# Moving the zero fills to a later pass, packing the routing logits and sharing softmax sums in a fused attention and two feed-forward kernel

## The chip, the cores and the metric

The kernel runs on one core of a Trainium2 chip. The metric is device time in microseconds (us) of one execution, as the median of several. Engines are TensorE (PE; its weight loads are PEld), VectorE (DVE), ScalarE (ACT), GpSimd (POOL) and SyncE (SP), which here only issues DMAs. Each engine works through its own list of instructions in order and waits where one needs something that is not there yet.

## What is computed

```
attn = softmax over the last 64 keys of q k^T / 8;  x = attn v      (4 batches, 8 heads, 576 x 64)
x    = reshaped to 2304 tokens x 512
h    = x w_in;  g = h tanh(softplus(h));  x = g w_out               (512 -> 2048 -> 512)
out  = x;  for tokens with x . w_skip > 0:
       e = argmax(x w_gate) of 8 experts, p its softmax weight
       out += p * relu(x w1[e]) w2[e]                               (512 -> 1024 -> 512)
```

The softmax divides by the sum plus 1e-9, in both places where one is taken.

## The kernel before

The 2304 tokens are six blocks of 384 (`NB`), each of three tiles of 128. A block passes through 16 chunks (`NF`) of the first feed-forward, 96 chunks in all. For chunk c, `L1` (L733) multiplies the block by 128 columns of w_in into an accumulator `ph`; seven small steps on VectorE and ScalarE make g of it (`m_min` L738, `m_exp` L741, `m_square` L745, `m_ln` L751, `m_r` L754, `m_g` L760, then a split into a high and a low part for blocks 1 to 5); `L2` (L784) adds its product with w_out into three accumulators po0, po1, po2, one for each tile. In block 0 the weights are also unpacked and split, by VectorE and ScalarE, and weights of w_out are read back by a DMA (`wide_back`, L677, tile ca). In that stage the attention of block 1 runs too, and so on, one block ahead. The attention of block 0 is the ramp ahead of chunk 0.

Attention goes by pairs of units (24 pairs, 48 units; a pair is two heads of a block): scores `sc` on TensorE (L504, 64x64 quadrants), masked row maxima on VectorE (`att_max`, L518), the sign flip of the maxima (`att_neg`, L523), exponentials with row sums on ScalarE (`att_exp`, L528), an addition and a reciprocal (L532, L535), the normalisation (L544), a transpose on TensorE (`tp`, L549), its copy PT, and the product with v (`pv`, L560). From pair 8 on q and k come transposed by VectorE (`dve_T`, L486 and L487) from tiles rq and rk, which SP loads.

After a block's last L2 its three tiles are evacuated (`x_evac`, L826 or L828) into tiles xs, of which there are three buffers, stored to the output, transposed (`rtp`, L839), copied to xf, and multiplied with [w_gate, w_skip] (`route_lg`, L852: four accumulating matmuls of a 128x128 float32 stationary and nine columns for each tile). `route_lge` (L857) copies the nine logits; the class `Group` makes of them a slot for every token, and an indirect DMA on GpSimd scatters the token to a slot table `xg_d` in DRAM (L272). Before the first scatter that table is filled with zeros: `fill_zero` (L263, L264) makes one zero tile zt in a buffer of the same three as xs, and `fill_store` (L267) stores it 16 times, 257 KB each, from GpSimd's queue. The second feed-forward runs at the end, expert by expert (L1182 to L1243).

The order on every engine comes from a planner (`Plan`). Each piece of work is a task with engines and costs (`one`, `two`), what it must follow (`after`), which buffers it takes (`get`) and uses, and a due time; `chunk_time(c)` is the planned time of chunk c. The planner takes the ready task that can start first and is due first, so a change of one due time or cost moves other instructions too. Tasks of the places below: `fz` and `fs` (zero tile and fills, L955 to L958), `xe` (evacuation), `rT`, `re`, `rl`, `lg` (routing, L975 to L983), `mx`, `ng`, `ex`, `ep`, `rc`, `nm`, `PT` (attention, L609 to L618). In gaps that the planner foresees in the ramp and at the end it puts small matmuls (`keep_warm`, L1136).

Of the kernel before, what the change touches and what calls it, by code (L numbers as in the profile page):

```python
# [169 lines left out]
def tile_kernel(  # L170
# [37 lines left out]
    def ctile(shape, dt, name):  # L208
        return cst.tile(shape, dt, tag=name, name=name)
# [26 lines left out]
    wgs = ctile([128, NK, NE + 1], F32, "wgs")  # L236
# [97 lines left out]
    def expert_L(eng, key):  # L334
# [22 lines left out]
                cv=2, ca=2, u=3, gHL=2, xs=3, xf=1, grp3=1, grp1=3)  # L357
# [4 lines left out]
    def one(eng, cost):  # L362
        return [(eng[0], eng[1], cost)]
# [143 lines left out]
    def att_max(u):  # L507
        sc = sc_t[u]
        first = [3 * g for g, _, _, s0 in runs(u // 8) if s0 == 0]
        if u in EXTRA:  # L510
            P = chp.tile([128, 3, 128], F32, tag="u", name="P", bufs=3)
        else:
            P = atp.tile([128, 3, 128], F32, tag="P", name="P")
        P_t[u] = P
        mx_t[u] = mx = atp.tile([128, 4, 3], F32, tag="mx", name="mx", bufs=4)
        for i in range(3):
            mask = [mask_first[w % 2] for w in first if w // 2 == i] or [maskA]
            V.tensor_tensor_reduce(P[:, i], sc[:, i], mask[0],  # L518
                                   op0=ALU.add, op1=ALU.max, scale=1.0, scalar=-3.0e38,
                                   accum_out=mx[:, 0, i:i + 1])  # L520

    def att_neg(u):
        V.tensor_scalar(mx_t[u][:, 1], mx_t[u][:, 0], -0.125, None, op0=ALU.mult)  # L523

    def att_exp(u):
        P, mx = P_t[u], mx_t[u]
        for i in range(3):
            A.activation(P[:, i], P[:, i], AF.Exp, bias=mx[:, 1, i:i + 1], scale=0.125,  # L528
                         accum_out=mx[:, 2, i:i + 1])

    def att_eps(u):
        V.tensor_scalar(mx_t[u][:, 2], mx_t[u][:, 2], 1e-9, None, op0=ALU.add)  # L532

    def att_rec(u):
        V.reciprocal(mx_t[u][:, 3], mx_t[u][:, 2])  # L535

    def att_norm(eng, u):
        P, mx = P_t[u], mx_t[u]
        if eng is A:
            for i in range(3):  # L540
                A.activation(P[:, i], P[:, i], AF.Copy, scale=mx[:, 3, i:i + 1])
        else:
            r = mx[:, 3].rearrange("p (a o) -> p a o", o=1).to_broadcast([128, 3, 128])
            eng.tensor_tensor(P, P, r, op=ALU.mult)  # L544
# [47 lines left out]
    for pr in range(NU // 2):  # L592
# [16 lines left out]
        for j in range(2):  # L609
            u = 2 * pr + j  # L610
            T(("mx", u), one(VV, .64), lambda e, u=u: att_max(u), after=[("S", pr)], get=[("u" if u in EXTRA else "P", ("P", u))],
              use=[("sc", u)])
            T(("ng", u), one(VV, .07), lambda e, u=u: att_neg(u), after=[("mx", u)])
            T(("ex", u), one(AA, 1.16), lambda e, u=u: att_exp(u), after=[("ng", u)])
            T(("ep", u), one(VV, .07), lambda e, u=u: att_eps(u), after=[("ex", u)])
            T(("rc", u), one(VV, .09), lambda e, u=u: att_rec(u), after=[("ep", u)])
            T(("nm", u), two(1.16, .47), lambda e, u=u: att_norm(e, u), after=[("rc", u)])
            T(("PT", u), one(PP, .36), lambda e, u=u: att_PT(u), after=[("nm", u)] + [("PV", pr - 1)] * (pr > 0),  # L618
              get=[("ps", ("tp", u))],
              use=[("P", u)])  # L620
            T(("Pe", u), two(.38, .47), lambda e, u=u: att_PTe(e, u), after=[("PT", u)], get=[("PT", ("PT", u))],
              use=[("tp", u)])
# [198 lines left out]
    xs_t, xf_t, lg_t, lp_t, sel_t, slot_t = ({} for _ in range(6))  # L821
# [26 lines left out]

    def route_lg(m, t):
        lp_t[m, t] = lp = ps_s.tile([128, NE + 1], F32, tag="ps", name="lp")  # L850
        for kk in range(NK):
            PE.matmul(lp, xf_t[m, t][:, kk], wgs[:, kk], start=kk == 0, stop=kk == NK - 1)  # L852

    def route_lge(m, t):
        if t == 0:
            lg_t[m] = sml.tile([128, 3, NE + 1], F32, tag="lg", name="lg", bufs=1)
        V.tensor_copy(lg_t[m][:, t], lp_t[m, t])  # L857
# [108 lines left out]
    for m in range(NB):  # L966
# [3 lines left out]
        for t in range(3):  # L970
# [422 lines left out]
```

## Time and profile before

| what | value |
|---|---|
| median of 3 runs | 718.08 us (717.58 to 719.88) |
| the profiled execution, its own time | 716.83 us |
| its span, first to last instruction | 715.1 us |
| PE, PEld busy | 689.8, 592.7 us |
| DVE, ACT, POOL busy | 457.0, 390.4, 74.2 us |
| moved by DMA | 92.54 MB |

The span is the time between the first and the last instruction in the trace; the time around it belongs to the start and end of the execution. Busy time of an engine is the union of its instructions' records; records of one engine overlap a little, since the next instruction starts before the last one's end has drained, so a group's cost is read from its start to the start of the next group. The clock is TensorE's granted clock as a share of its upper level, 2.4 GHz; 0.5 is the lower level, 1.2 GHz.

### The profile page before, as it was taken

How to read it: one execution, taken by the hardware profiler on the slowest of the kernel's cores; microseconds unless marked ns; L12 is line 12 of the kernel's file. 1: busy time of each engine (PE TensorE's matmuls, PEld its weight loads, DVE VectorE, ACT ScalarE, POOL GpSimd, SP SyncE). 2: the span in 40 equal slices, each digit the busy share in tenths (PEclk: the TensorE clock that was granted, in tenths of full speed). 3: DMA queues.
4: the chain of work that ended last, by engine and by line, in shares of the span. 5: the costliest groups of instructions: out<-in, count | busy, mean ns of one | idle time of the engine just before them, and what ended most of it. 6: DMA issues, size and time to landing. Idle time of an engine off the chain costs nothing.

```text
span 715.1 us, 13649 instructions
## 1 busy us (share of the span) xinstructions
PE 689.8 (96%) x4904; PEld 592.7 (83%) x4904; DVE 457.0 (64%) x1353; ACT 390.4 (55%) x955; POOL 74.2 (10%) x138
## 2 busy tenths in 40 slices
PE   7999997999999999999999999999989999999995
PEld 7776665688888888888888888889978988898983
DVE  5899995887567656665666745546567363564351
ACT  5887774676566666556666665656544243222130
POOL 2000050000020001000020001002233111020011
PEclk9999998999999999999999999999999999999998
DMA  7889998652122213231210300054464677678100
GB/s 174 209 223 272 289 322 193 146 168 73 37 67 59 63 36 72 49 82 30 47 34 21 96 1 9 18 162 133 132 184 146 200 262 251 233 278 300 60 24 20
DMA packets 141645, 92.54 MB, mean 129 GB/s; under 512 B 110189, under 2 KB 118381, under 8 KB 141568
## 3 DMA queue, kind: packets, MB, share of 16 engines
q1 hardware_dynamic: 137568, 82.90, 41.1%
q0 software_dynamic: 4000, 8.63, 3.5%
q8 instruction: 45, 0.74, 0.4%
q14 instruction: 32, 0.26, 0.1%
HBM read 73.96 MB, written 17.86 MB: 128 GB/s over the span
## 4 chain that ended last, share of the span: by engine, by line
PE 56%; issue 16%; DMA 13%; SPq 7%; DVE 4%; POOL 2%; ACT 1%; POOLq 0%; DVEq 0%; ACTq 0%
PE ph L733 23%; PE po L784 23%; DMA w<-in_moe_w_in_dram 4%; DMA vt<-in_v_dram 4%; DMA st<-in_moe_w_dram 2%; PE pv L560 2%; PE lp L852 2%; POOL out_dram L287 2%; PE sc L504 2%; SPq L406 2%; PE tp L549 1%; DMA ca<-w 1%; SPq L420 1%; PE rtp L839 1%; DMA xg<-xg_d 1%
## 5 line engine op out<-in xcount | busy, mean ns | idle before, releaser
L733 PE MATMUL ph<-xH,w 128*128 128x384 f32 x768 | 222.9, 351 | 3.7 <-DVE g L760 2.1
L784 PE MATMUL po<-w,gH 128*128 128x512 f32 x480 | 153.0, 400 | 0.0
L733 PEld LDWEIGHTS ph<-xH,w 128*128 128x128 f32 x768 | 142.1, 189 | 11.8 <-DVE g L760 4.4
L733 PE MATMUL ph<-xL,w 128*128 128x384 f32 x384 | 130.8, 341 | 0.0
L741 ACT ACTIVATE u<-u 128x384 f32<-128x384 f32 x96 | 50.1, 522 | 115.8 <-DVE u L738 103.1
L784 PEld LDWEIGHTS po<-w,gH 128*128 128x128 f32 x480 | 88.1, 188 | 14.5
L784 PE MATMUL po<-w,gL 128*128 128x512 f32 x240 | 95.1, 396 | 0.3 <-DVE gL L769 0.3
L760 DVE SCALAR_TENSOR_TENSOR u<-u,ph 128x384 f32<-128x384 f32 x80 | 44.1, 551 | 60.9 <-ACT u L754 60.4
L733 PEld LDWEIGHTS ph<-xL,w 128*128 128x128 f32 x384 | 72.8, 190 | 2.0 <-issue 1.1
L738 DVE TENSOR_SCALAR u<-ph 128x384 f32<-128x384 f32 x96 | 53.1, 553 | 20.6 <-PE ph L733 20.0
L1182 PEld LDWEIGHTS ph<-xgT,w 128*128 128x128 f32 x512 | 63.7, 190 | 0.9 <-issue 0.3
L1182 PE MATMUL ph<-xgT,w 128*128 128x144 f32 x512 | 64.1, 286 | 0.2 <-issue 0.2
L528 ACT ACTIVATE P<-P,mx 128x128 f32<-128x128 f32 x144 | 55.7, 388 | 7.3 <-DVE mx L523 7.3
L784 PEld LDWEIGHTS po<-w,gL 128*128 128x128 f32 x240 | 45.1, 188 | 12.5 <-DVE gL L769 1.6
L751 ACT ACTIVATE u<-u 128x384 f32<-128x384 f32 x96 | 50.2, 522 | 2.4
L754 ACT ACTIVATE u<-u 128x384 f32<-128x384 f32 x96 | 50.1, 522 | 2.3
L745 ACT ACTIVATE u<-u 128x384 f32<-128x384 f32 x96 | 50.0, 521 | 2.3
L769 DVE TENSOR_TENSOR gL<-u,gH 128x384 fp32r<-128x384 f32 x80 | 47.5, 593 | 3.7 <-ACT gH L310 1.4
L1209 ACT ACTIVATE hH<-ph 128x288 fp32r<-128x288 f32 x32 | 13.2, 411 | 62.3 <-PE ph L1182 43.4
L784 PE MATMUL po<-w,g 128*128 128x512 f32 x96 | 44.4, 598 | 1.0 <-DVE w L669 1.0
L1226 PE MATMUL po<-w,hH 128*128 128x512 f32 x128 | 42.6, 414 | 0.0
L272 POOL DMA_INDIRECT xg_d<-xs,r_si x18 | 18.5, 1030 | 157.0 <-DVE mx L518 77.0
(149 smaller groups left out, 1028.7 us busy)
## 6 DMA issues: line engine op xcount, KB each, us to landing
st<-in_moe_w_dram SPq DMA_DIRECT2D x64, 256.0 KB
w<-in_moe_w_dram SPq DMA_DIRECT2D x32, 512.0 KB
w<-in_moe_w_in_dram SPq DMA_DIRECT2D x16, 512.0 KB
w<-in_moe_w_out_dram SPq DMA_DIRECT2D x16, 512.0 KB
out_dram<-xs SPq DMA_DIRECT2D x18, 256.0 KB
xg_d<-zt POOLq DMA_DIRECT2D x16, 257.0 KB
xg<-xg_d SPq DMA_DIRECT2D x16, 257.0 KB
ca<-w SPq DMA_DIRECT2D x16, 256.0 KB
```

Of the source, the lines that this page charges most:

```text
L528: A.activation(P[:, i], P[:, i], AF.Exp, bias=mx[:, 1, i:i + 1], scale=0.125, accum_out=mx[:, 2, i:i + 1])
L733: PE.matmul(phs[c], a[:, kk], b[:, kk], start=kk == 0 and n == 0, stop=kk == NK - 1 and n == len(terms) - 1)
L738: V.tensor_scalar(u, phs[c], 20.0, None, op0=ALU.min)
L741: A.activation(us[c], us[c], AF.Exp)
L745: A.activation(us[c], us[c], AF.Square, bias=1.0)
L751: A.activation(us[c], us[c], AF.Ln, scale=0.5, bias=half_t[c])
L754: A.activation(us[c], us[c], AF.Exp, scale=-1.0)
L760: V.scalar_tensor_tensor(o, us[c], 1.0, phs[c], op0=ALU.subtract, op1=ALU.mult)
L769: eng.tensor_tensor(gL, us[c], gH.bitcast(F32), op=ALU.subtract)
L784: PE.matmul(po[m, t], a[:, ts], b, start=f == 0 and n == 0, stop=f == NF - 1 and n == len(terms) - 1)
L1182: PE.matmul(ph[:, i], w1_t[e, kk][:, 128 * f:128 * f + 128], xgT[e][:, kk, :N1], start=kk == 0, stop=kk == NK - 1)
L1226: PE.matmul(po2[e, s], a[:, f, ss], b, start=f == 0 and n == 0, stop=f == 7 and n == 2)
```

## The change

Three things, and the planner's new order that follows from them.

- The zero tile and its 16 fills are due at chunks 17 and 18 and after, where they were due at chunks 11 and 13.
- Routing of blocks 0 to 4: for each tile four matmuls with the stationary weights padded to 32 columns (`wgs`, now 128x4x32, zeroed first) write four column quarters of one tile `lq`, one per slice of 128 features; `route_fewe` copies it out, and for each block three matmuls with a constant `sum4` add the four parts and bring the tokens back to the partitions (`route_sum`). One copy of the logits serves a block. Block 5 keeps the old way.
- Softmax: the masked scores are multiplied by -0.125 and their minimum is taken, so the sign flip is gone; maxima and sums of a pair lie in one tile, and the addition and the reciprocal are made once for the pair.

```
-    wgs = ctile([128, NK, NE + 1], F32, "wgs")
+    wgs = ctile([128, NK, 32], F32, "wgs")
+    G.memset(wgs, 0.0)
+    sum4 = ctile([128, NE + 1], F32, "sum4")
+    for p0 in range(0, 128, 32):
+        G.tensor_copy(sum4[p0:p0 + 32], ident[p0:p0 + 32, p0:p0 + NE + 1])
...
             V.tensor_tensor_reduce(P[:, i], sc[:, i], mask[0],
-                                   op0=ALU.add, op1=ALU.max, scale=1.0, scalar=-3.0e38,
-                                   accum_out=mx[:, 0, i:i + 1])
-    def att_neg(u):
-        V.tensor_scalar(mx_t[u][:, 1], mx_t[u][:, 0], -0.125, None, op0=ALU.mult)
+                                   op0=ALU.add, op1=ALU.min, scale=-0.125, scalar=3.0e38,
+                                   accum_out=mx[:, 0, u % 2, i:i + 1])
...
-            A.activation(P[:, i], P[:, i], AF.Exp, bias=mx[:, 1, i:i + 1], scale=0.125,
-                         accum_out=mx[:, 2, i:i + 1])
+            A.activation(P[:, i], P[:, i], AF.Exp, bias=mx[:, 0, u % 2, i:i + 1], scale=-1.0,
+                         accum_out=mx[:, 1, u % 2, i:i + 1])
-    def att_eps(u):
-        V.tensor_scalar(mx_t[u][:, 2], mx_t[u][:, 2], 1e-9, None, op0=ALU.add)
-    def att_rec(u):
-        V.reciprocal(mx_t[u][:, 3], mx_t[u][:, 2])
+    def att_eps(pr):
+        V.tensor_scalar(mx_t[pr][:, 1], mx_t[pr][:, 1], 1e-9, None, op0=ALU.add)
+    def att_rec(pr):
+        V.reciprocal(mx_t[pr][:, 2], mx_t[pr][:, 1])
...
-            T(("ng", u), one(VV, .07), lambda e, u=u: att_neg(u), after=[("mx", u)])
-            T(("ep", u), one(VV, .07), lambda e, u=u: att_eps(u), after=[("ex", u)])
-            T(("rc", u), one(VV, .09), lambda e, u=u: att_rec(u), after=[("ep", u)])
+        T(("ep", pr), one(VV, .07), lambda e, pr=pr: att_eps(pr), after=[("ex", 2 * pr), ("ex", 2 * pr + 1)])
+        T(("rc", pr), one(VV, .09), lambda e, pr=pr: att_rec(pr), after=[("ep", pr)])
...
+    def route_few(m, t):
+        lq_t[m, t] = lq = ps_s.tile([128, 128], F32, tag="ps", name="lq")
+        for kk in range(NK):
+            PE.matmul(lq[32 * kk:32 * kk + 32], wgs[:, kk], xf_t[m, t][:, kk], start=True, stop=True)
+    def route_fewe(eng, m, t):
+        if t == 0:
+            lq_t[m] = sml.tile([128, 3, 128], F32, tag="lq", name="lqs", bufs=1)
+        copy(eng, lq_t[m][:, t], lq_t[m, t])
+    def route_sum(m):
+        lp_t[m] = lp = ps_s.tile([128, 3, NE + 1], F32, tag="ps", name="lp")
+        for t in range(3):
+            PE.matmul(lp[:, t], lq_t[m][:, t], sum4, start=True, stop=True)
-    def route_lge(m, t):
-        if t == 0:
-            lg_t[m] = sml.tile([128, 3, NE + 1], F32, tag="lg", name="lg", bufs=1)
-        V.tensor_copy(lg_t[m][:, t], lp_t[m, t])
+    def route_lge(m):
+        lg_t[m] = sml.tile([128, 3, NE + 1], F32, tag="lg", name="lg", bufs=1)
+        V.tensor_copy(lg_t[m], lp_t[m])
...
-    T(("fz",), one(VV, .55), lambda e: fill_zero(), get=[("xs", "zt")], due=chunk_time(11), t0=chunk_time(10))
+    T(("fz",), one(VV, .55), lambda e: fill_zero(), get=[("xs", "zt")], due=chunk_time(17), t0=chunk_time(17))
...
-          lat=6, due=chunk_time(13) + 1.0 * n)
+          lat=6, due=chunk_time(18) + 1.0 * n)
```

Where it moves instructions. On VectorE, in block 0's pass, the memset of the zero tile (zt) stood between two steps of the weight unpacking (ca, cv, w) before:

```order
L760 SCALAR_TENSOR_TENSOR g<-u,ph 128x384
L654 SCALAR_TENSOR_TENSOR ca<-w_1438,cv 128x512
L263 MEMSET zt 128x513
L264 MEMSET zt 128x1
L654 SCALAR_TENSOR_TENSOR ca<-w_1303,cv 128x512
L671 ISA ca<-ca,cv 128x1024
```

Now it stands behind the transposes for pair 10 and ahead of the normalisations (P) of a pair whose transposes stand between block 0's last two L2 groups on TensorE:

```order
L742 TENSOR_SCALAR u<-ph 128x384
L490 STREAM_TRANSPOSE kT<-rk 128x448
L491 STREAM_TRANSPOSE qT<-rq 128x384
L535 TENSOR_SCALAR mx<-mx 128x6
L267 MEMSET zt 128x513
L268 MEMSET zt 128x1
L538 RECIPROCAL mx<-mx 128x6
L697 TENSOR_TENSOR w_1914<-ca,w_1914 128x512
L547 TENSOR_TENSOR P<-P,mx 128x384 x2
```

It moved by some 50 instructions, from about chunk 10 to about chunk 15 of block 0. On ScalarE, at the border of blocks 0 and 1, the three evacuations xs stood together before, ahead of chunk 18's four steps on u:

```order
L754 ACTIVATE u<-u 128x384
L826 ACTIVATE xs<-po 128x512 x3
L310 ACTIVATE w_2143<-ca 128x512
L741 ACTIVATE u<-u 128x384
L745 ACTIVATE u<-u 128x384
```

Now the third, whose buffer is that of zt, comes after three exponentials and three of chunk 18's four steps:

```order
L830 ACTIVATE xs<-po 128x512 x2
L314 ACTIVATE w_2101<-ca 128x512
L745 ACTIVATE u<-u 128x384
L749 ACTIVATE u<-u 128x384
L531 ACTIVATE P,mx<-P,mx 128x128 x3
L755 ACTIVATE u<-u 128x384
L830 ACTIVATE xs<-po 128x512
L758 ACTIVATE u<-u 128x384
```

On GpSimd the fills (xg_d<-zt) stood among memsets of v tiles and ahead of the three small copies into xs:

```order
L396 MEMSET vt 64x128
L267 DMA xg_d<-zt 128x514 x15
L471 MEMSET rk 128x64
L830 COPY xs<-tok 128x1 x3
```

Now the copies, which follow the evacuations, come between the fills:

```order
L475 MEMSET rk 128x64
L271 DMA xg_d<-zt 128x514 x11
L834 COPY xs<-tok 128x1
L271 DMA xg_d<-zt 128x514
L834 COPY xs<-tok 128x1
L271 DMA xg_d<-zt 128x514 x4
L834 COPY xs<-tok 128x1
```

So the third copy and the third evacuation are behind all 16 fills, which nothing waited for at that place before.

## Rows read from the trace of the kernel before

**Rows 1.** The page, part 1: busy us, share of the span, instructions.
```profile
PE 689.8 (96%) x4904; PEld 592.7 (83%) x4904; DVE 457.0 (64%) x1353; ACT 390.4 (55%) x955; POOL 74.2 (10%) x138
```

**Rows 2.** Busy time by stage: window, length; PE, PEld, DVE, ACT, POOL; clock, DMA.
```profile
46.00:104.00 58.00, 56.65 (x336) 39.14 (x336) 57.17 (x155) 45.92 (x110) 7.12 (x14) 1.00 0.98 280
104.00:109.00 5.00, 4.56 (x18) 3.32 (x19) 2.13 (x7) 2.20 (x9) 2.21 (x5) 1.00 1.12 305
109.00:122.00 13.00, 8.53 (x69) 7.01 (x68) 7.95 (x16) 5.33 (x11) 0.74 (x5) 0.74 0.81 180
122.00:146.00 24.00, 23.11 (x109) 15.28 (x108) 20.36 (x56) 15.96 (x39) 0.00 (x0) 1.00 0.61 146
146.00:525.00 379.00, 379.00 (x2612) 333.90 (x2611) 242.45 (x770) 231.62 (x578) 30.10 (x49) 1.00 0.26 67
```

**Rows 3.** Waits from 84 to 136 us: us in total, times, longest.
```profile
DVE kT L486 <- DMA rk<-in_k_dram: 5.2, 1, 5.2
```

**Rows 4.** Timeline of VectorE: start, us, instruction, idle time before it.
```profile
111.35 0.65 DVE L486 STREAM_TRANSPOSE kT<-rk 128x448 f32<-128x448 f32 x1 [5.22 <-DMA rk<-in_k_dram]
...
113.01 0.55 DVE L544 TENSOR_TENSOR P<-P,mx 128x384 f32<-128x384 f32 x1
```

**Rows 5.** Timeline of TensorE at the stall.
```profile
109.25 0.49 PE L549 MATMUL tp<-ident,P 128*128 128x128 f32 x3
113.71 0.87 PE L549 MATMUL tp<-ident,P 128*128 128x128 f32 x3 [3.97 <-DVE P L544]
114.23 0.67 PE L733 MATMUL ph<-xH,w 128*128 128x384 f32 x1
...
118.35 1.53 PE L560 MATMUL pv<-PT,vt 128*64 128x64 f32 x24
```

**Rows 6.** The chain of waits: an L2 and an L1 group at full clock.
```profile
143.36 2.57 PE po L784 x6
145.93 2.12 PE ph L733 x12
```

**Rows 7.** Timeline of GpSimd: first and last fill issue, and who waits.
```profile
93.94 0.76 POOL L267 DMA_DIRECT2D xg_d<-zt  x1 [39.00 <-DMA vt<-in_v_dram]
...
106.86 0.54 POOL L267 DMA_DIRECT2D xg_d<-zt  x1 [0.19 <-issue]
...
114.51 0.18 POOL L830 COPY xs<-tok 128x1 int32<-128x1 int32 x1 [2.00 <-DMA xg_d<-zt]
```

**Rows 8.** DMA queues from 88 to 115 us: packets, MB, share of 16 engines.
```profile
q1 hardware_dynamic: 9332, 4.04, 58.9%
q0 software_dynamic: 1280, 4.21, 47.9%
```

**Rows 9.** Timeline of TensorE in block 1: transposes, score and logit groups.
```profile
168.80 0.60 PE L839 MATMUL rtp<-ident,xs 128*128 128x128 f32 x4
169.15 0.71 PE L784 MATMUL po<-w,gH 128*128 128x512 f32 x2
...
171.43 0.89 PE L504 MATMUL sc<-kT,qT 64*64 64x128 f32 x24
172.25 0.44 PE L733 MATMUL ph<-xH,w 128*128 128x384 f32 x1
...
176.58 0.96 PE L852 MATMUL lp<-wgs,xf 128*128 128x9 f32 x8
177.39 0.42 PE L733 MATMUL ph<-xH,w 128*128 128x384 f32 x1
```

**Rows 10.** The tile mx: count, duration ns min/median/max.
```profile
L523 DVE TENSOR_SCALAR mx<-mx x48: 139/161/396, 11.7 to 445.5; 128x3 f32<-128x3 f32 x48
L532 DVE TENSOR_SCALAR mx<-mx x48: 125/163/318, 15.1 to 449.4; 128x3 f32<-128x3 f32 x48
L535 DVE RECIPROCAL mx<-mx x48: 131/176/178, 15.8 to 449.5; 128x3 f32<-128x3 f32 x48
```

**Rows 11.** Groups by line: busy us, mean ns of one score pass.
```profile
L504 PE MATMUL sc<-kT,qT 64*64 64x128 f32 x576 | 21.7, 277 | 1.9 <-ACT qT L310 1.2 <-issue 0.7
```

More of the change, by code (lines that the diff above doesn't have):

```diff
@@ L356, in tile_kernel @@
     BUFS = dict(ps=3, ph=2, po0=1, po1=1, po2=1, rk=4, rq=2, vt=3, kT=2, qT=2, P=2, PT=2, xHL=2,
-                cv=2, ca=2, u=3, gHL=2, xs=3, xf=1, grp3=1, grp1=3)
+                cv=2, ca=2, u=3, gHL=2, xs=3, xf=1, grp3=1, grp1=3, lqs=1)
     plan = Plan(BUFS)
@@ L514, in att_max @@
         P_t[u] = P
-        mx_t[u] = mx = atp.tile([128, 4, 3], F32, tag="mx", name="mx", bufs=4)
+        if u % 2 == 0:
+            mx_t[u // 2] = atp.tile([128, 3, 2, 3], F32, tag="mx", name="mx", bufs=3)
+        mx = mx_t[u // 2]
         for i in range(3):
@@ L612, in tile_kernel @@
               use=[("sc", u)])
-            T(("ng", u), one(VV, .07), lambda e, u=u: att_neg(u), after=[("mx", u)])
-            T(("ex", u), one(AA, 1.16), lambda e, u=u: att_exp(u), after=[("ng", u)])
-            T(("ep", u), one(VV, .07), lambda e, u=u: att_eps(u), after=[("ex", u)])
-            T(("rc", u), one(VV, .09), lambda e, u=u: att_rec(u), after=[("ep", u)])
-            T(("nm", u), two(1.16, .47), lambda e, u=u: att_norm(e, u), after=[("rc", u)])
+            T(("ex", u), one(AA, 1.16), lambda e, u=u: att_exp(u), after=[("mx", u)])
+        T(("ep", pr), one(VV, .07), lambda e, pr=pr: att_eps(pr), after=[("ex", 2 * pr), ("ex", 2 * pr + 1)])
+        T(("rc", pr), one(VV, .09), lambda e, pr=pr: att_rec(pr), after=[("ep", pr)])
+        for j in range(2):
+            u = 2 * pr + j
+            T(("nm", u), two(1.16, .47), lambda e, u=u: att_norm(e, u), after=[("rc", pr)])
             T(("PT", u), one(PP, .36), lambda e, u=u: att_PT(u), after=[("nm", u)] + [("PV", pr - 1)] * (pr > 0),
@@ L818, in tile_kernel @@
               use=[("gHL", c)], due=chunk_time(NC + 1) + LO + .01 * t)
-    xs_t, xf_t, lg_t, lp_t, sel_t, slot_t = ({} for _ in range(6))
+    xs_t, xf_t, lg_t, lp_t, lq_t, sel_t, slot_t = ({} for _ in range(7))
     def x_evac(eng, m, t):
@@ L851, in route_lg @@
         for kk in range(NK):
-            PE.matmul(lp, xf_t[m, t][:, kk], wgs[:, kk], start=kk == 0, stop=kk == NK - 1)
-    def route_lge(m, t):
-        if t == 0:
-            lg_t[m] = sml.tile([128, 3, NE + 1], F32, tag="lg", name="lg", bufs=1)
-        V.tensor_copy(lg_t[m][:, t], lp_t[m, t])
+            PE.matmul(lp, xf_t[m, t][:, kk], wgs[:, kk, :NE + 1], start=kk == 0, stop=kk == NK - 1)
+    def route_lge(m):
+        lg_t[m] = sml.tile([128, 3, NE + 1], F32, tag="lg", name="lg", bufs=1)
+        V.tensor_copy(lg_t[m], lp_t[m])
     class Group:
@@ L978, in tile_kernel @@
               get=[("rk" if last else "xf", ("xf", m, t))], use=[("rtp", m, t)])
+            if not last:
+                T(("rl", m, t), one(PP, .25), lambda e, m=m, t=t: route_few(m, t), after=[("re", m, t), ("wg",)],
+                  get=[("ps", ("lq", m, t))], use=[("xf", m, t)], due=tb + dt * (3 + 2 * t))
+                T(("rq", m, t), two(.22, .19), lambda e, m=m, t=t: route_fewe(e, m, t), after=[("rl", m, t)],
+                  use=[("lq", m, t)], get=[("lqs", ("lqs", m))] if t == 0 else ())
+                continue
             T(("rl", m, t), one(PP, .75), lambda e, m=m, t=t: route_lg(m, t), after=[("re", m, t), ("wg",)],
               get=[("ps", ("lp", m, t))], use=[("xf", m, t)], due=tb + dt * (3 + 2 * t))
-            if not last:
-                T(("lg", m, t), one(VV, .08), lambda e, m=m, t=t: route_lge(m, t), after=[("rl", m, t)],
-                  use=[("lp", m, t)])
+        if not last:
+            T(("rs", m), one(PP, .66), lambda e, m=m: route_sum(m), after=[("rq", m, t) for t in range(3)],
+              get=[("ps", ("lp", m))], use=[("lqs", m)], due=tb + dt * 8.5)
+            T(("lg", m), one(VV, .1), lambda e, m=m: route_lge(m), after=[("rs", m)], use=[("lp", m)])
         prev = None
@@ L986, in tile_kernel @@
             g = Group(m, t0, n)
-            lgs = [("lg", m, t0 + t) if n > 1 else ("rl", m, t0) for t in range(n)]
+            lgs = [("lg", m) if n > 1 else ("rl", m, t0)]
             lu = [("lp", m, t0)] if n == 1 else []
```

8 lines of the change are left out of this document (4 added, 4 removed).

## Prediction

> **What bounds the kernel now.** I read the engines' busy time first, then busy time by stage, then the waits of the worst stage, then single instructions there. TensorE is busy for 689.8 us of a span of 715.1 [rows 1]. By stage the picture splits [rows 2]: from 146 to 525 us (blocks 1 to 5 of the first feed-forward) TensorE has no gap at all at full clock, while VectorE is busy 64% and ScalarE 61%. What is taken from TensorE there shortens the run one for one; what is taken from the others is worth nothing. From 46 to 104 us (block 0) TensorE, VectorE and the DMA engines are all full (56.7 and 57.2 of 58 us, DMA share 0.98): no single engine is the bound. Then the stage breaks: from 104 to 122 us TensorE idles 0.44 + 4.47 us, its clock falls to 0.74 of full speed, and VectorE idles 2.87 + 5.05 us.
>
> Why it breaks is in the waits and the timelines. VectorE stood 5.2 us before its transposes of kT, for the DMA that brings rk [rows 3, 4]. The second normalisation of an attention pair stands behind these transposes in VectorE's order; TensorE, which needs it to transpose P, stood 3.97 us [rows 5]. After that idle time its matmuls ran at half speed: the L1 group that starts at 114.23 and ends at 118.35 took 4.12 us, such a group takes 2.12 at full clock [rows 5, 6]. The DMA was late because the 16 fills of the slot table were issued from 93.94 to 107.4 us, and the next instruction that waits for the last of them ran at 114.51 [rows 7]; of the DMA time between 88 and 115 us the fills took 47.9%, everything else 58.9% [rows 8].
>
> **The change part by part.** The sum is made against the profiled execution: span 715.1, time 716.83. The median of the three runs, 718.08, is 1.25 above it; I add that at the end.
>
> *Fills leave block 0.* They are now issued after a memset near the end of block 0's pass, 16 issues on GpSimd's queue as before. What they leave behind is the broken stretch. TensorE idled 4.47 us from 109 to 122 and lost (1 - 0.74) x 13 = 3.4 us to the clock; with the small gaps on either side (0.44 and 0.89) that is 9.2 us at most [rows 2]. VectorE could give back the 7.9 us that it idled. Not all of it returns, for VectorE is full before and 85% busy after (20.36 of 24 us [rows 2]); its order becomes the next thing that is late. I take 7 us, with 3.5 (half) and 9.2 as ends.
>
> *Fills arrive at the border of blocks 0 and 1.* The zero tile takes one of three buffers; the third evacuation of block 0's output needs that same buffer and waits for all 16 fills. It stands in ScalarE's order between two steps of chunk 18, and TensorE's L2 of chunk 16 needs the accumulator that it frees. From the memset's end TensorE has this to do before it stands there: about 2 us until both normalisations are done (0.55 each [rows 4] and two shorter instructions), six transposes 0.8 (0.49 for three [rows 5]), L1 2.12, a pv group 0.9, L2 2.57, L1 2.12, a score group 0.82, L1 2.12, transposes 0.35, two thirds of an L2, 1.4: 15.2 us [rows 6, 9], the pv group priced like a score group's record. The pv group waits for two copies that stand behind four activations of chunk 16 on ScalarE; I put 1.5 us on that. So TensorE arrives after some 16.7 us, and with 0.6 for the evacuation the fills must have landed by 16. Before they took 20.6 us from first issue to release [rows 7]; their packets alone need 0.479 x 27 = 12.9 us of the DMA engines [rows 8], and others use 0.61 of them in the stage that precedes the border [rows 2]. I take 18 us: 2 us late, 1.5 for the pv group, 0.5 for the queue behind. Cost 4 us; ends 0 (landing by 14) and 9.5 (landing after 20.6, 4.6 us idle, with 3.4 us of slow clock behind it as now, and the 1.5). GpSimd has nothing else due then; the loads on SP's queue share the DMA with the fills, and their covers are conversions placed some four chunks ahead of their use.
>
> *Routing.* A tile's four logit matmuls (eight passes) hold TensorE 0.81 us: start 176.58, next group 177.39 [rows 9]. There are 15 such tiles in blocks 0 to 4, all in the full stage: 12.15 us go. Instead each tile has four matmuls of 32 columns on four column quarters (eight passes of 128 moving columns), and each block three summing matmuls (six passes of the old kind, 0.1 each): 5 x 0.6 = 3.0 us. No column quarter is in the trace. Nearest is the score group on 64x64 quadrants, four at a time: 24 passes in 0.82 us [rows 9], 0.034 a pass, so 0.27 a tile. The other end is no overlap, at the rate of the transposes of 128 columns, 0.35 for four [rows 9], 0.7 a tile. I take 0.35, near the quadrants, as they are the same kind of sharing: 15 x 0.35 + 3.0 - 12.15 = -3.9 us; ends -5.1 and +1.35. The Trainium skill ("TensorEngine Tiling (Array Packing)", Key Properties) speaks against the change: a switch of tiling mode drains the engine, and every new group switches twice. The score group's 0.82 already holds two switches, so by the row they cost little; if each had to be paid on top, at the 0.15 us by which the record of an old logit group outlasts its 0.81, the sum would be 15 x 0.57 + 3.0 - 12.15 = -0.6 instead of -5.1. Evacuating the quarters (128x128, on ScalarE or VectorE) is covered by the 36 to 39% that these idle there.
>
> *Softmax.* Per pair of units two sign flips, one addition and one reciprocal leave VectorE: 96 instructions in all, of 0.16 to 0.18 us each [rows 10], overlapping. Sixteen of the 24 pairs run where TensorE is full and VectorE is not: worth nothing. In the ramp and block 0 there are at most 4 x 4 in a stage, 16 x 0.16 = 2.6 us of VectorE time beside full TensorE. The price is that the first unit's sum waits for the second unit's exponentials. I take -0.3 us, for ramp and block 0 together; ends -1 and +1. The extra memset and copies at the start are on GpSimd, before it is waited for.
>
> Sum: -7 + 4 - 3.9 - 0.3 = -7.2. Profiled 709.6, median 718.08 - 7.2 = **710.9**.
>
> **The rivals.** A run of this kernel can tell about 0.3% from no change: 715.9 to 720.2.
>
> (1) *The border costs what block 0 gains.* Fills take their old 20.6 us, TensorE idles over 4 us, the clock falls again: 9.5 instead of 4, 716.4. For it: others already use 0.61 of the DMA, and the old stall of 3.97 us did drop the clock. Against: there are fewer small packets at the border than at 94 us. It decides from a landing some 20 us after the memset. Chance 0.17.
>
> (2) *VectorE is the bound of block 0.* Without the DMA wait TensorE waits for g and for normalisations instead; half returns: 714.4. For it: VectorE has no idle time to speak of from 46 to 104. Against: TensorE has none either. Chance 0.13.
>
> (3) *Everything works.* Fills land in time, quarters overlap like quadrants: -9.2 - 5.1 - 0.3 = -14.6, 703.5. Chance 0.12.
>
> (4) *Quarters do not run side by side*, though the source says so: 0.7 a tile, +1.35 in place of -3.9: 716.1. Chance 0.05.
>
> (5) *Slower:* each pass on a quarter runs to its end before the next starts, at the 0.277 us that a score pass lasts by itself [rows 11]. Then 8 x 0.277 = 2.2 us a tile in the full stage, 15 x 2.216 + 3.0 - 12.15 = +24.1 in place of -3.9: 738.9. It decides from 0.83 us a tile, where the 3.3 us net of the other parts are spent. For it: no row shows matmuls on quarters; against: the score group, whose passes overlap four at a time. Chance 0.05.
>
> **How the numbers follow.** The forecast keeps 0.48. Faster by over 0.3%: forecast, (2), (3) and half of (1), 0.48 + 0.13 + 0.12 + 0.08 = 0.81. Within 0.3%: the other half of (1), and (4): 0.14. Slower: (5), 0.05. The range for 8 in 10 runs from 703.5 (rival 3) to 716.6 (rivals 1 and 4), which leaves out rival 5 and the outer parts of 1 and 3.
>
> **What would show it.** In the changed profile: no wait of VectorE for rk over 1 us near 105 to 112 us, and full clock from 100 to 130; a wait of ScalarE's third xs evacuation for the fills, with TensorE idle 1 to 4 us behind it and the clock at most briefly low; routing groups lq of 0.3 to 0.45 us from start to next start, lp groups of 0.6 per block; the stage of blocks 1 to 5 shorter by 3 to 5 us. Wrong would be: the same idle TensorE in block 0 with no fills near it, a border stall of over 5 us, or lq groups above 0.7 us.

## The result, and the profile after

The changed kernel takes 712.75 us (median of 4 runs, 712.09 to 713.92), the kernel before 718.98 in the same series: ratio 0.9915, 95% interval 0.9888 to 0.9941, 6.2 us faster where 7.2 were forecast (the forecast for the median was 710.9). A second series gave 0.9899 (0.9874 to 0.9924). The profiled execution is one of 712.69 us, span 710.9. The page's part 1, against [rows 1], has 4.5 us less of TensorE and 12.8 less of VectorE:

```profile
PE 685.3 (96%) x4921; PEld 584.8 (82%) x4921; DVE 444.2 (62%) x1247; ACT 396.7 (56%) x973; POOL 76.8 (11%) x144
```

Busy time by stage (columns as in [rows 2]):

```profile
46.00:104.00 58.00, 57.94 (x346) 40.45 (x345) 57.25 (x147) 47.59 (x116) 0.35 (x2) 1.00 0.89 254
104.00:109.00 5.00, 4.70 (x41) 3.25 (x40) 5.00 (x11) 3.37 (x8) 0.00 (x0) 1.00 0.60 143
109.00:122.00 13.00, 13.00 (x72) 8.96 (x71) 12.33 (x35) 9.23 (x25) 0.16 (x1) 1.00 0.69 146
122.00:140.00 18.00, 15.34 (x106) 10.90 (x104) 9.83 (x23) 9.17 (x20) 9.42 (x18) 1.00 0.99 308
140.00:160.00 20.00, 17.85 (x76) 15.67 (x77) 16.64 (x45) 11.19 (x30) 0.34 (x2) 0.83 0.55 176
160.00:515.00 355.00, 355.00 (x2515) 307.21 (x2514) 212.23 (x648) 224.64 (x557) 27.68 (x47) 1.00 0.25 62
515.00:565.00 50.00, 45.69 (x301) 41.66 (x299) 27.51 (x96) 17.49 (x36) 14.54 (x15) 0.93 0.50 165
```

The broken stretch of block 0 is gone: from 104 to 122 us TensorE idles 0.3 us where it idled 4.9, its clock is full, and VectorE is busy 17.33 of 18 us. A new broken stretch stands at the border, 122 to 160 us: TensorE idles 2.66 and 2.15 us, VectorE 8.2 of 18 us and ScalarE 8.8 in the first half, and the clock is 0.83 in the second, a mean of both levels. The waits between 118 and 160 us (us in total, times, longest) say for what:

```profile
DVE w L316 <- DMA ca<-w: 8.2, 3, 4.9
POOL xs L834 <- DMA xg_d<-zt: 7.6, 1, 7.6
ACT w L314 <- DMA ca<-w: 4.5, 2, 4.1
...
PE ph L737 <- DVE u L764: 3.0, 1, 3.0
...
PE po L788 <- ACT xs L830: 1.8, 1, 1.8
```

And the timelines of the four engines there, first VectorE, then ScalarE, TensorE and GpSimd:

```profile
135.28 0.43 DVE L316 CAST w<-ca 128x512 fp32r<-128x512 f32 x1 [4.87 <-DMA ca<-w]
135.63 0.55 DVE L742 TENSOR_SCALAR u<-ph 128x384 f32<-128x384 f32 x1
...
136.21 0.53 ACT L745 ACTIVATE u<-u 128x384 f32<-128x384 f32 x1 [6.39 <-DVE u L742]
...
143.74 0.63 ACT L314 ACTIVATE w<-ca 128x512 fp32r<-128x512 f32 x1 [4.14 <-DMA ca<-w]
...
147.31 0.57 ACT L830 ACTIVATE xs<-po 128x512 f32<-128x512 f32 x1
...
140.37 0.44 PE L737 MATMUL ph<-xH,w 128*128 128x384 f32 x1 [3.03 <-DVE u L764]
...
147.94 1.12 PE L788 MATMUL po<-w,gH 128*128 128x512 f32 x2 [1.78 <-ACT xs L830]
...
151.69 0.63 PE L788 MATMUL po<-w,gH 128*128 128x512 f32 x2
...
134.10 0.54 POOL L271 DMA_DIRECT2D xg_d<-zt  x1 [0.17 <-issue]
142.22 0.18 POOL L834 COPY xs<-tok 128x1 int32<-128x1 int32 x1 [7.58 <-DMA xg_d<-zt]
```

Read them from VectorE on. It stands 4.87 us for a read-back of w_out (tile ca), then makes the first step of chunk 17 (L742); ScalarE has waited 6.39 us for that step; TensorE waits 3.03 us for the g that comes out of the chain. Then ScalarE itself stands 4.14 us for another read-back, and its third evacuation, which comes behind, runs at 147.31. The fills had landed 5 us earlier: the copy that waits for them runs at 142.22, 19.3 us after the zero tile's memset ended (122.95). So what came late was not what the forecast had pointed at: no row has ScalarE waiting for the fills. After the two stops the L2 pairs at 147.94 take twice what the pair at 151.69 takes (1.12 and 0.63). The late reads were slow from issue to landing: of the 16 read-backs issued between 88 and 165 us half landed within 2.4 us, and the slowest took 9.6. The reason is the one that [rows 8] gave for rk: from 122 to 146 us the fills hold half of the DMA time (packets, MB, share):

```profile
q0 software_dynamic: 1280, 4.21, 49.3%
q1 hardware_dynamic: 5856, 2.79, 41.6%
```

Routing, against [rows 9]: a tile's logit group takes 0.36 us to the next start where it took 0.81, the three summing matmuls 0.69:

```profile
162.43 0.43 PE L857 MATMUL lq<-xf,wgs 128*32 128x128 f32 x8
162.79 0.44 PE L737 MATMUL ph<-xH,w 128*128 128x384 f32 x1
...
189.40 0.84 PE L868 MATMUL lp<-sum,lqs 128*128 128x9 f32 x6
190.09 0.42 PE L737 MATMUL ph<-xH,w 128*128 128x384 f32 x1
```

There is one new loss that no step of the forecast named, at the end of the first feed-forward. ScalarE stands for st, the staged weights of the second feed-forward, with the steps of a u behind it, and TensorE waits 3.04 us, then runs its next group slowly:

```profile
530.79 0.63 ACT L314 ACTIVATE w<-st 128x512 fp32r<-128x512 f32 x1 [6.59 <-DMA st<-in_moe_w_dram]
...
534.13 2.07 PE L1062 MATMUL sel<-ident,base 128*128 128x128 f32 x8 [3.04 <-DVE u L764]
```

**A table by stage.** Up to the end of a block every kernel of this study has nearly the same work behind it on TensorE, so the stages can be divided at the L2 groups of the last chunk of a block: the start of whatever follows that group on TensorE. In the timeline after, L2 of chunk 15 starts at 131.57 and the next group at 133.85. The last column is what is left of the span; the ratio is that to the kernel before, with its interval, each in its own series.

| kernel | ratio (95%) | to the end of L2(0) | to L2(15): block 0 | to L2(31): border and block 1 | to L2(79): blocks 2 to 4 | rest |
|---|---|---|---|---|---|---|
| before | 1 | 50.7 | 94.6 | 82.1 | 246.2 | 241.5 |
| the change | 0.9915 (0.9888 to 0.9941) | 49.5 | 84.3 | 89.7 | 244.0 | 243.3 |
| e0, the change again | 0.9899 (0.9874 to 0.9924) | 51.5 | 84.2 | 88.6 | 244.0 | 245.8 |
| e1, fills alone | 1.0014 (0.9998 to 1.003) | 51.2 | 91.4 | 89.4 | 246.2 | 239.8 |
| e2, routing alone | 0.9951 (0.993 to 0.9972) | 50.6 | 94.5 | 81.4 | 244.0 | 242.2 |
| e3, softmax alone | 0.9992 (0.9975 to 1.0008) | 51.7 | 94.7 | 82.1 | 246.1 | 240.6 |
| e4, change, fills back | 0.9967 (0.995 to 0.9984) | 50.7 | 92.9 | 81.4 | 244.0 | 243.4 |
| e5, zero tile in xf | 0.9908 (0.988 to 0.9935) | 53.3 | 84.1 | 88.4 | 244.2 | 245.6 |
| e6, and fills late | 0.9838 (0.9809 to 0.9867) | 53.8 | 84.2 | 83.1 | 244.1 | 242.4 |
| e7, lq twice | 0.9947 (0.9928 to 0.9967) | 50.0 | 84.4 | 88.9 | 246.0 | 244.8 |
| e8, before, fills late | 0.9866 (0.9844 to 0.9888) | 51.1 | 86.6 | 82.0 | 246.2 | 242.6 |
| e9, late, behind routing | 0.9839 (0.9809 to 0.9868) | 53.1 | 84.2 | 81.6 | 244.2 | 244.5 |
| e10, late, 32 fills | 1.0325 (1.0301 to 1.035) | 52.2 | 84.2 | 81.6 | 282.8 | 241.5 |
| e11, late, 24 fills | 0.9826 (0.9788 to 0.9863) | 51.8 | 84.2 | 81.6 | 244.2 | 242.8 |

The three middle columns repeat to some tenths of a us between kernels that share the part in question, except where fills stand at the border; the first and the last differ by 2 to 2.5 us between two executions of the same kernel (the change and e0), so nothing under 2 us is read from a single pair there. The trace of the kernel before is of an execution that took 716.83 us, 1 to 3 us under the medians of its series; where stages add up to less than the ratios say (in e8 6.6 against 9.6 us), this is part of it.

### The profile page after: what moved, and what is told of

The parts are those of the page before. It is cut to its first block, busy times and chain, and to the rows that moved or that the text cites. A ratio compares the mean times of both kernels' runs of the same rounds, so it can differ in the third digit from the quotient of the medians.

```text
span 710.9 us, 13617 instructions
## 1 busy us (share of the span) xinstructions
PE 685.3 (96%) x4921; PEld 584.8 (82%) x4921; DVE 444.2 (62%) x1247; ACT 396.7 (56%) x973; POOL 76.8 (11%) x144
## 4 chain that ended last, share of the span: by engine, by line
PE 76%; issue 7%; DMA 6%; DVE 4%; ACT 2%; SPq 2%; POOL 1%; POOLq 0%; DVEq 0%; ACTq 0%
PE po L788 27%; PE ph L737 26%; PE ph L1209 7%; PE po L1253 4%; PE sc L508 2%; PE pv L563 2%; DMA ca<-w 2%; DMA st<-in_moe_w_dram 2%; PE tp L552 2%; DMA w<-in_moe_w_in_dram 1%; PE rtp L843 1%; DMA vt<-in_v_dram 1%; PE po L1268 1%; PE lq L857 1%; POOL out_dram L291 1%
## 5 line engine op out<-in xcount | busy, mean ns | idle before, releaser
L788 PE MATMUL po<-w,gH 128*128 128x512 f32 x480 | 154.7, 404 | 1.8 <-ACT xs L830 1.8
L745 ACT ACTIVATE u<-u 128x384 f32<-128x384 f32 x96 | 50.0, 521 | 94.7 <-DVE u L742 94.6
L742 DVE TENSOR_SCALAR u<-ph 128x384 f32<-128x384 f32 x96 | 53.0, 553 | 25.9 <-PE ph L737 25.7
L788 PEld LDWEIGHTS po<-w,gL 128*128 128x128 f32 x240 | 45.7, 190 | 11.6 <-DVE gL L773 0.7
```

The lines of the kernel that those rows point to most:

```text
L742: V.tensor_scalar(u, phs[c], 20.0, None, op0=ALU.min)
L745: A.activation(us[c], us[c], AF.Exp)
L788: PE.matmul(po[m, t], a[:, ts], b, start=f == 0 and n == 0, stop=f == NF - 1 and n == len(terms) - 1)
```

## The experiments

**Each part alone.** e1 is the kernel before with the two due times of the change; e2 with its routing, e3 with its softmax; e4 is the change with the due times of before.

```
-    T(("fz",), ..., due=chunk_time(11), t0=chunk_time(10))
+    T(("fz",), ..., due=chunk_time(17), t0=chunk_time(17))
-          lat=6, due=chunk_time(13) + 1.0 * n)
+          lat=6, due=chunk_time(18) + 1.0 * n)
```

> The kernel before with the due times of the zero tile and the fills of the change, nothing else. My theory: the stall of block 0 is the fills' alone, and the price at the border is the fills' too. Then L2 of chunk 15 ends 8 to 11 us earlier than before (145.4 there), TensorE idles 4 to 6 us between chunks 15 and 19 with a slow clock behind it, and some 2 to 3 us of gain are left: ratio 0.996 to 0.998. Rival: the stall of block 0 went because the softmax lost 96 instructions of VectorE in the change; then VectorE is late here without a DMA, L2 of chunk 15 ends at most 5 us earlier, the border is paid in full, and the kernel is slower by 2 to 5 us: ratio 1.003 to 1.007.

It came out between the two, with no difference that is clear of noise (1.0014, interval 0.9998 to 1.003). TensorE stood twice at the border, each time behind VectorE's waits for read-backs, and the first of these stops comes right behind L2 of chunk 15, so the table counts it with block 0. Without its 3.02 us block 0 gave back 6.2 (94.6 to 88.4), and the border took 10.3 (82.1 to 89.4, and those 3.02):

```profile
142.65 0.59 PE L733 MATMUL ph<-xH,w 128*128 128x384 f32 x1 [3.02 <-DVE u L760]
...
150.77 0.69 PE L733 MATMUL ph<-xH,w 128*128 128x384 f32 x1 [4.21 <-DVE u L760]
```

> The kernel before with the routing of the change, nothing else. My theory: TensorE has no gap from 146 to 525 us, so its own time counts one for one: an lq group 0.36 us, three summing matmuls 0.67 per block, 12.97 us of lp groups gone: -4.3 us, ratio 0.994, with the wait of VectorE for rk near 111 us as before. Rival: the gain in the full stage is given back by another order of VectorE and ScalarE at the end of the first feed-forward, as the wait of 3 us ahead of the sel matmuls in the changed kernel suggests: -1 to -2 us, ratio 0.997 to 0.999.

Ratio 0.9951: 3.5 us. 0.7 us of it are in block 1 (82.1 to 81.4) and 2.2 in blocks 2 to 4 (246.2 to 244.0), some 0.73 us a block, and the stall of block 0 is as it was:

```profile
114.65 0.52 PE L553 MATMUL tp<-ident,P 128*128 128x128 f32 x3 [4.67 <-DVE P L548]
```

The rival has something too: the rest does not get shorter though block 4's routing lies there (241.5, 242.2), and TensorE waits 2.72 us ahead of sel, as after the change.

> The kernel before with the softmax of the change, nothing else. My theory: worth 1.2 us in the ramp (the first L1 group starts at 44.73 in the changed kernel and at 45.95 before) and nothing behind it; the wait for rk near 111 us and TensorE's stall there stay: -0.3 to -1.5 us, ratio 0.998 to 1.000. Rival: the normalisation that is now made for a pair is what freed block 0; then the stall of 3.97 us before the transposes of P is gone here too, with the clock full, and the ratio is 0.988 to 0.992.

0.9992, no measurable gain, and block 0 takes 94.7 us as before. But the stall is not the same one. Up to L2 of chunk 9 this kernel needs 51.6 us from L2(0), the one before 53.7, so the softmax does save 2.1 us there. Then the L2 of chunk 12 waits 6.75 us for its weights (w, the last step of their unpacking on VectorE), where before the transposes of P waited 3.97 [rows 5]. The unpacking is late because VectorE stood twice for rk, as it did once before [rows 3], and ScalarE for a read-back:

```profile
114.85 0.65 DVE L486 STREAM_TRANSPOSE kT<-rk 128x448 f32<-128x448 f32 x1 [4.09 <-DMA rk<-in_k_dram]
...
120.23 0.65 DVE L486 STREAM_TRANSPOSE kT<-rk 128x448 f32<-128x448 f32 x1 [3.37 <-DMA rk<-in_k_dram]
...
120.51 0.63 ACT L310 ACTIVATE w<-ca 128x512 fp32r<-128x512 f32 x1 [9.06 <-DMA ca<-w]
...
125.59 4.54 PE L784 MATMUL po<-w,g 128*128 128x512 f32 x6 [6.75 <-DVE w L669]
```

> The changed kernel with the zero tile and the fills due at chunks 11 and 13 again. My theory: the wait for rk comes back near 105 to 112 us (4 to 6 us), the border is clean, and what is left is routing and softmax: 4.3 to 5.5 us faster than the kernel before, ratio 0.992 to 0.994, so that moving the fills is worth no more than 1 to 3 us in the change. Rival: block 0 is freed by routing and softmax, the fills cost nothing there now: 10 us or more faster, ratio 0.986 or less, better than the change.

2.4 us faster than before, less than I expected and far from the rival's 10. Block 0 takes 92.9 us, and the fills still hold it: VectorE's wait for rk is back, 5.76 us, if later than expected, and L2 of chunk 12 waits 5.65 us for the unpacking behind it, as in e3:

```profile
117.47 0.65 DVE L490 STREAM_TRANSPOSE kT<-rk 128x448 f32<-128x448 f32 x1 [5.76 <-DMA rk<-in_k_dram]
...
122.62 4.76 PE L788 MATMUL po<-w,g 128*128 128x512 f32 x6 [5.65 <-DVE w L673]
```

Beside the change (0.9915, 0.9899) the ratio of 0.9967 puts the move of the fills at 3.7 to 4.9 us once routing and softmax are there, more than the 1 to 3 expected. The two traces show only 1.6 of it (spans 712.5 and 710.9; 8.6 won in block 0, 8.3 lost behind it), since e4's is of one of its faster executions (714.25, median 716.86).

**What the border's price is made of.** e5 keeps the fills at the border and takes the shared buffer away: the zero tile goes into the buffer of xf, which is idle until the routing. e6 moves the fills into block 1 as well. e0 is the change itself in the same series.

```
-        zt[0] = xsp.tile([128, XW], F32, tag="xs", name="zt")
+        zt[0] = sml.tile([128, NK * 128 + 2], F32, tag="xf", name="zt", bufs=1)
...
-            xf = sml.tile([128, NK, 128], F32, tag="xf", name="xf", bufs=1)
+            xf = sml.tile([128, NK * 128 + 2], F32, tag="xf", name="xf", bufs=1)[:, :NK * 128].rearrange("p (k n) -> p k n", k=NK)
...
-    T(("fz",), ..., get=[("xs", "zt")], due=chunk_time(17), t0=chunk_time(17))
+    T(("fz",), ..., get=[("xf", "zt")], due=chunk_time(17), t0=chunk_time(17))
```

> The changed kernel itself, unaltered, beside the three that follow. 712 to 714 us, ratio to the kernel before 0.990 to 0.993; in the trace again one idle stretch of TensorE of about 3 us before an L1 group near 140 us and one of 1 to 2.5 us before an L2 group near 148.

As expected in time, and at the lower end in ratio. Its idle stretches were 3.72 and 0.57 us, so the first one repeats and the second, the one that the forecast was about, is the smaller.

> The changed kernel with its zero tile in the buffer of xf (that of the routing, idle then) in place of the third buffer of xs; the fills keep their due times. The third evacuation no longer waits for the fills. My theory: most of the border's price is the read-backs of w_out (ca) that share the DMA engines with the fills; the idle 3 us before the L1 group and the waits of VectorE and ScalarE for ca (8 and 4 us) stay, only the 1.8 us before L2 and some of the slow clock behind it go: 2 to 4 us faster than the change, ratio to before 0.985 to 0.989. Rival: the shared buffer is the price, as the prediction had it; then the border is clean and it is 6 us or more faster than the change, ratio 0.983 or less.

No gain that can be seen: 713.2 beside e0's 713.41, each spread over some 5 us. No evacuation waits for the fills now, and still TensorE stands before an L2 group, because the evacuations come behind chunk 17's steps on ScalarE, and those behind VectorE's wait for a read-back. The waits from 118 to 160 us:

```profile
ACT u L745 <- DVE u L742: 11.1, 5, 7.7
DVE w L316 <- DMA ca<-w: 10.0, 4, 6.2
...
PE po L788 <- ACT xs L830: 4.2, 1, 4.2
```

So the rival, the buffer, falls. My own theory was wrong in size and place: the wait ahead of L1 went, and the one ahead of L2 stayed. In place of two stops of TensorE (3.03 and 1.78 us in the change, 3.72 and 0.57 in e0) there is one of 4.17, behind a wait of VectorE for a read-back that is now 6.2, and the clock from 140 to 160 us is 0.83 again.

In e6 the due times are `chunk_time(24)` for the tile and `chunk_time(25) + 1.0 * n` for the fills.

> The same with the zero tile due at chunk 24 and the fills from chunk 25, in block 1, where the DMA share is 0.25 to 0.3 and no read-back of weights is due. My theory: no stall in block 0 (as in the change), none at the border, and the first scatters move behind the fills at no cost: 6 to 9 us faster than the change, ratio to before 0.978 to 0.983. Rival: wherever 4.2 MB of fills go something waits for them; the scatters hold the three xs tiles until the next block's evacuations (chunk 32), TensorE stands there for 2 us or more, and it is no more than 3 us faster than the change, ratio 0.987 or more.

4.5 us faster than e0 (708.9, 713.41), between theory and rival in time. The border is clean (83.1 against 88.6), and the one idle stretch left is that an xf had to wait for the fills in the buffer that they share:

```profile
180.85 0.43 PE L857 MATMUL lq<-xf,wgs 128*32 128x128 f32 x8 [1.43 <-ACT xf L314]
```

**The fills by themselves.** e8 puts the same late fills into the kernel before, e9 into the change, both with the zero tile made behind block 0's last logit group (`after=[("rl", 0, 2)]` at fz).

> The kernel before, softmax and routing as they were, with the zero tile in the buffer of xf, due at chunk 24 and made behind block 0's last logit group, and the fills from chunk 25. It prices the fills by themselves, at a place where nothing waits for what shares the DMA engines with them. My theory: the stall of block 0 (9 us with its slow clock) is the fills' alone; 6 to 8 us faster than before, ratio 0.989 to 0.992, no wait of TensorE over 2 us between 46 and 200 us. Rival: block 0 needs the softmax of the change too, as the fills alone at the border gave nothing: 0 to 3 us faster, ratio 0.996 or more, with TensorE waiting over 2 us for VectorE or ScalarE in block 0.

Ratio 0.9866, 9.6 us by the ratio, a little over my bound; 8.0 of it in block 0 (94.6 to 86.6), with nothing lost at the border (82.0). The rival falls. Busy time by stage in e8:

```profile
46.00:122.00 76.00, 74.69 (x452) 52.34 (x453) 74.45 (x204) 58.81 (x146) 1.03 (x7) 1.00 0.86 228
122.00:160.00 38.00, 36.92 (x234) 29.03 (x233) 32.90 (x85) 25.82 (x59) 0.35 (x2) 1.00 0.49 142
```

> The late fills of the changed kernel, with the zero tile made behind block 0's last logit group, so that no xf has to wait for the fills (TensorE stood 1.43 us for that). My theory: 0.5 to 2 us faster than that, ratio to before 0.980 to 0.983, no idle TensorE from 120 to 500 us. Rival: the fills, now later, hold up the scatters and with them block 1's evacuations: an idle stretch of 1 us or more near chunk 32 (220 to 230 us), ratio 0.984 or more.

In time it equals e6 (0.9839, 0.9838); in the stage it is 1.5 us shorter (81.6, 83.1), and there is no idle TensorE from 120 to 515 us. It is the kernel to keep: 11.6 us faster than before by the ratio, and some 4.5 faster than the change. Over e8 the ratio gains 2 us, and the two intervals overlap; the three middle stages are 4.8 us shorter, but in these two traces the first stage and the rest are 3.9 longer.

```profile
122.00:160.00 38.00, 38.00 (x245) 30.59 (x246) 32.91 (x89) 26.86 (x69) 0.35 (x2) 1.00 0.53 151
160.00:200.00 40.00, 40.00 (x304) 33.94 (x304) 27.27 (x94) 24.46 (x65) 12.15 (x21) 1.00 0.66 161
200.00:515.00 315.00, 315.00 (x2192) 273.29 (x2187) 187.81 (x562) 198.20 (x489) 25.95 (x42) 1.00 0.25 64
```

**Does block 1 have room?** e10 issues every fill of e9 twice in a row; e11 issues the sixteen and then the first eight again.

> The same with every fill issued twice, 32 in place of 16, the same zeros again. It asks whether the place in block 1 has room or was only just wide enough. My theory: nothing on the path waits for a transfer there, so 4.2 MB more cost 0 to 1 us. Rival: 4.2 MB cost some 5 to 8 us of TensorE at any place where the DMA engines are shared with loads that are needed soon, as in block 0 and at the border; then 4 us or more slower than with 16.

This missed its question. Each second store writes the rows of the one before it and waits for that to land (16 waits, 58.2 us in all), so 32 stores took from 171.67 to 247.57 us, the scatters waited, block 0's xs tiles stayed taken, and TensorE stood 34.02 us for the evacuations of block 1. What it does show is the place's last moment: from 221.2 us on TensorE stands.

```profile
255.22 1.22 PE L789 MATMUL po<-w,gH 128*128 128x512 f32 x2 [34.02 <-DVE xs L833]
```

> The late fills behind the routing, with the first eight rows of tiles filled a second time after all sixteen: 24 stores, none of which waits for one to the same rows just before it (which is what drew the run with 32 in pairs out past the scatters' last moment). TensorE's order up to the second feed-forward is that of the run with 16. My theory: in block 1 nothing on the path waits for the DMA engines, so 2.1 MB more cost nothing: within 1.5 us of the run with 16, no idle TensorE from 120 to 500 us, scatters some 8 to 11 us later (194.3 with 16). Rival: the bytes themselves cost time wherever they go, 2.5 to 4 us for half as many again (7 to 10 us for 16 in block 0): ratio to before 0.987 or more, with TensorE waiting behind a late load between 180 and 215 us.

705.77 us, ratio 0.9826, beside e9's 0.9839: no price. With the DMA share at 0.99 for 20 us TensorE has no gap:

```profile
180.00:200.00 20.00, 20.00 (x152) 17.33 (x151) 13.15 (x55) 12.37 (x32) 8.23 (x17) 1.00 0.99 261
```

The first scatter went at 200.22 us (194.3 in e9), some 6 us later. The rival, that bytes cost time wherever they go, falls.

**The price of column quarters.** e7 writes every group of four quarters a second time.

```
-        for kk in range(NK):
+        for kk in [*range(NK), *range(NK)]:
```

> The changed kernel with every group of four logit matmuls on column quarters issued twice, with the same results written again: 15 groups of four more. It prices the passes without the switch into and out of the mode. My theory: the 0.36 us of a group is mostly its eight passes, four side by side, with little for the switch; a second set costs 0.2 to 0.3 us, 3 to 4.5 us in all, ratio to the change 1.004 to 1.006. Rival, by the rule that a switch of mode drains the engine: over half of the 0.36 is the switch, a second set costs 0.1 to 0.15, 1.5 to 2.2 us in all, ratio 1.002 to 1.003, lq groups 0.46 to 0.51 from start to next start.

2.8 us slower than e0 (716.22, 713.41). A doubled group takes 0.58 us to the next start, a single one 0.36, so a second set of eight passes, without any switch, costs 0.22 us, and 0.14 are left for the group's beginning and end. The theory holds for the group (its total, 3 to 4.5 us, is a little above the 2.8); the rival, 0.46 to 0.51, falls:

```profile
161.60 0.64 PE L857 MATMUL lq<-xf,wgs 128*32 128x128 f32 x16
162.18 0.44 PE L737 MATMUL ph<-xH,w 128*128 128x384 f32 x1
```

In the table the three blocks with nine groups between L2(31) and L2(79) are 2.0 us longer (244.0 to 246.0), 0.22 a group again.

## Why the prediction was right, and where it was not

The sign and the size hold, 6.2 us for 7.2, but two terms were too small and one was missing: block 0 gave more, the border took more, and the end gave some back. That these errors cancel to within 1 us is luck; between the two traces that the terms are read from, the gain is 4.2 us.

*Fills leave block 0: -7 forecast, 8.0 measured without the rest of the change (e8), 10.3 in the change (94.6 to 84.3).* The mechanism is shown: the fills late and nothing else, and block 0's stall is gone. The bound that VectorE's fullness set (rival 2, half returns) is out. What went over the upper end of 9.2 is the next point.

*Softmax: -0.3 forecast with -1 as the end, about -2.4 in block 0.* Alone it gives nothing (e3), and with the fills out of the way block 0 takes 84.2 us with it (e9) and 86.6 without (e8). The step that failed is the pricing of VectorE's 2.6 us as beside the path because TensorE was full as well: in e8 TensorE stands 0.75 and 1.05 us in block 0 for VectorE's g and w, in e9 it does not wait for VectorE there at all, and that is 1.8 of the 2.4. While the fills stood in block 0, whatever was won ahead of them was waited away at the next late read (6.75 us in e3).

*Border: +4 forecast, about +8.1 measured (89.7 against 81.6 in e9).* This is the largest error, and the failed step is a sentence: that SP's loads share the DMA with the fills, "and their covers are conversions placed some four chunks ahead of their use". That protects TensorE's use of the weights, and not the engines that convert them: VectorE and ScalarE stand at the conversion in their own order, and the steps of u behind it are on TensorE's path. The landing was forecast well (18 us after the memset, 19.3 measured), but the wait built on it, the third evacuation's, was not the cause: without it the time is the same (e5), and the sign named for it, ScalarE waiting for the fills, is not in the trace. In size, TensorE's standing was near the forecast (2.66 + 2.15 = 4.8 us); what the 4 left out is the clock, (1 - 0.83) x 20 = 3.4 us. Rival 1 had the price nearly right (9.5, with such a clock) and the cause wrong.

So 16 fills cost 8.0 us in block 0 and 8.1 at the border of the change: moving them there was worth nothing by itself (e1). The change is faster by routing and by what softmax gives once block 0 is clean; that fits e4, where the move is worth 3.7 us or more with both of them there.

*Routing: -3.9 forecast; summed over TensorE's groups from start to next start, -4.3:* 15 lq groups take 5.34 us (0.356 each, 0.35 forecast), the sums 3.35 (0.67 a block, 0.6 forecast), and 12.98 of lp groups are gone, where 12.15 were put down because the group read was one of 0.81 and eight of the 15 took 0.91. By stages it is 0.73 a block, some 3.7; the difference of the two countings is not resolved. Rivals 4 and 5 are out. The sum that paid two switches of 0.15 on top of 0.27 a tile came to -0.6, and the trace says -4.3. The Trainium skill ("TensorEngine Tiling (Array Packing)", Key Properties) says that a change of tiling mode drains the engine. The 0.14 us that a group costs beside its passes leaves room for that, inside the 0.36; no row shows the drain itself.

*Missing: the end.* The rest of the span is 1.8 us longer in the change than before though a block's routing was taken from it. One pair says little, but the 14 traces agree once they are sorted by the mean clock that was granted from 515 to 565 us (in e10, which is late, from 547 to 597). At 0.97 the rest is 239.8 to 241.5 us with the old routing (before, e1, e3) and 241.5 to 242.8 with the new (e2, e6, e10, e11); at 0.93 it is 242.6 (e8) and 243.3 to 244.8 (the change, e4, e7, e9); at 0.86 245.6 and 245.8 (e5, e0). So most of the spread goes with the clock, and at equal clock the new routing is 1 to 2 us longer. The row of before, for the one of the change above:

```profile
515.00:565.00 50.00, 46.45 (x307) 41.43 (x306) 30.69 (x104) 20.47 (x42) 16.43 (x16) 0.97 0.45 143
```

In the change TensorE's idle time and slow group ahead of sel stand behind ScalarE's wait for st. Such a stop of 2.4 to 3.7 us ahead of sel is in every kernel with the new routing, and in none with the old, whose longest stop near there is 1.6 to 1.8 us. It is not that a faster first feed-forward meets the staged weights sooner: e8 ends it 6 us earlier than before and stops 1.78 us (before 1.69), e10 ends it 32 us later than the change and still stops 2.37. It goes with the order that the new routing brings; which instruction of that order does it, no run shows.

*The sum by stages:* -1.2 to the end of L2(0), -10.3 in block 0, +7.6 at the border and in block 1, -2.2 in blocks 2 to 4, +1.8 in the rest: -4.3, and the two spans differ by 4.2. The medians differ by 6.2: the profiled execution of before, at 716.83, is 2.2 under the median of its series, 718.98, and that of the change, at 712.69, is at its own. The first and last terms are within what two executions of one kernel differ by.

Open: why the move cost more in e1 than in the change. Against the same kernels with the fills late (e8, e9) it took 4.8 us in block 0 and 7.4 behind it in e1, 0.1 and 8.1 in the change; TensorE's two stops are 3.02 and 4.21 us there, 3.03 and 1.78 here. Open too: what in the new order makes the stop ahead of sel.

## What to carry to other kernels

A bulk transfer that nobody waits for soon still costs what it delays: before moving one, list the loads that are in flight there and which engine's queue stands at their first use, not only when the last engine needs the result. Place it where no load is due soon and ahead of its own last moment; that alone was worth 9.6 us here by the ratio (e8), more than the whole change. A saving ahead of a stall on a transfer is waited away at that stall, so parts measured one by one do not add up to the whole.

## What the runs showed of the hardware that was not expected

A DMA share of 0.99 for 20 us is harmless in one place (e11, 180 to 200 us, TensorE 20.00 of 20) and goes with a border 8 us longer in another (the change, 122 to 140 us, share 0.99, TensorE 15.34 of 18): the share alone does not give the price.

Four 128x32 quarters in float32, 128 moving columns: a second set of eight passes right behind the first adds 0.22 us (e7), a group with all that surrounds it takes 0.36.

An idle stretch of 1.43 us left the clock full (e6: 1.00 in all stages from 104 to 240 us); 3.03, 3.72 and 4.17 us at the border (the change, e0, e5) each left it at 0.83 between 140 and 160 us, a mean of stretches at the upper and the lower level. The length of a stop does not settle it: at the end of the first feed-forward 2.92 us left the clock full (e6, 1.00 from 527 to 539 us), and 1.78 us came with 0.86 (e8, 524 to 536).
